# A fused attention and gated-unit kernel: other buffers, a replanned order, and the last stores spread over three queues

## The chip, the cores and the metric

The kernel runs on one core of a Trainium2 chip. The time is device microseconds (us) of one execution; a median is given with its range. The kernel before takes 337.1 us (336.81 to 337.18, four runs).

The engines are called as the profile calls them: PE is TensorE, PEld its weight loads, DVE is VectorE, ACT is ScalarE, POOL is GpSimd, SP is SyncE. A "q" behind a name (POOLq, SPq) is that engine's sequencer, which issues transfers. "The span" is the time from the first to the last instruction in a trace. E is the moment when PE has finished its last matmul.

## The reference, cut to what matters

Eight batches of 576 tokens, eight heads of 64 columns, all in fp32:

```
kv   = einsum('bhsd,bhse->bhde', k, v)          # 64 x 64 per head
out  = einsum('bhsd,bhde->bhse', q, kv)         # "raw" in the kernel
x    = out / sqrt(mean(out^2) + 1e-6) * g_norm  # then heads side by side: (8, 576, 512)
gate = sigmoid(causal convolution of x, 5 taps, per column)
y    = (gate * (x @ w_val)) @ w_out
```

## The kernel before

A planner is given every step with an engine, a wanted time, a duration, and what it needs and frees. It sorts the steps into one order per engine; a table of shifts, found by a search, moves the wanted times. Three parts matter here.

The loads. Half of k (four heads) is one tile; first halves have two buffers (2 - 0), second halves one (2 - 1). All go over SyncE's queue.

```python
    def load_half(name, src, b, i):
        t = loads.tile([P, H // 2, NJ, D], FP32, tag=f"{name}{i}", bufs=2 - i, name=f"{name}{i}_{b}")
        nc.sync.dma_start(out=..., in_=src[b, i * H // 2:(i + 1) * H // 2, 0:SF, :]...)
```

The turn of x. VectorE transposes 32 x 32 blocks into a tile y, and GpSimd's transfers move them into xT.

```python
    def turn_blocks(b, c):
        if ("y", b) not in st:
            st["y", b] = work.tile([P, C // TB, NJ, TB], FP32, tag="y", bufs=1, name=f"y{b}")
        nc.vector.transpose(out=st["y", b][:, :, c, :], in_=...)
```

The stores. A row block of 128 x 512 results (`ot`) leaves in four stores of 64 KB, all over SyncE's queue:

```python
    def store(i, c):
        ot = st["ot", i, c]
        for j in range(HB):                      # HB = 4
            ...
            nc.sync.dma_start(out=rows_out[2 * i + bb, n], in_=ot[j * TB:(j + 1) * TB, :])
```

The last pair of row blocks of the last batch is made by seven products (`fast_product` 0 to 6, lines "cb" and "a" in the profile), whose results ScalarE copies and VectorE adds. One more product ("single", lines "out") makes the last short row block.

Of the kernel before, what the change touches and what calls it, by code (L numbers as in the profile page):

```python
# [18 lines left out]


SHIFTS = {
    "fast_product": {0: -31.5, 1: 1.5, 2: -4},
    "gate_tap": {0: 13, 1: 77, 2: 43, 3: 77, 4: 87, 5: 70.5, 6: 69.5, 7: 67.5},
    "keep_x": {0: -25},
    "kv_product": {5: -4.5, 6: -4.5, 7: -10.5},
    "load_half": {("k", 0): 7.5, ("k", 1): 13.5, ("k", 3): 6.5, ("k", 4): -7, ("k", 5): 34.5,
        ("k", 6): 3.5, ("v", 0): -60.5, ("v", 1): 19.5, ("v", 2): 27.5, ("v", 4): 13, ("v", 5): -9.5,
        ("v", 6): 3, ("v", 7): 9.5},
    "load_q": {4: -11.5, 5: -12, 6: -14.5, 7: -11.5},
    "load_tails": {4: 4.5, 5: -101.5, 6: -108.5},  # L30
    "narrow_weight": {("wout", 0): 36, ("wout", 1): 20.5, ("wout", 3): -39},
    "normalise": {7: 10.5},
    "out_product": {1: 38.5, 3: -6},
    "raw_product": {4: -84, 5: -23, 6: -17.5},
    "square": {2: -9},
    "stage_weight": {("cw", 0): -235.5, ("wout", 0): 13, ("wout", 1): 22, ("wout", 3): -4,
        ("wval", 2): -117, ("wval", 3): -123.5},
    "store": {0: 57.5},
    "sums": {2: 9.5, 5: -91},
    "token_sums": {0: 11.5},  # L40
    "turn_blocks": {6: 23, 7: 9},
    "turn_q": {2: 5.5, 3: 27.5},
    "turn_x": {1: 3, 3: 7.5},
    "val_fast": {7: 12.5},
    "val_product": {0: 33.5, 1: 23, 3: 8.5},
    "weight_sums": {0: 35.5},
    "x_sums": {6: -9},
}


# [85 lines left out]
def kernel(  # L136
# [67 lines left out]
    def ps(kind, shape, name):  # L204
        return psum.tile(shape, FP32, tag=kind, bufs=BANKS[kind], name=name)

    plan = Planner({
        "k0": 2, "k1": 1, "v0": 2, "v1": 1, "tails": 2, "q": 3, "w64": 3, "y": 1, "wexp": 2,
        "kv": 1, "kvbd": 2, "qT": 2, "tp": 1, "raw": 2, "mm": 4, "sq": 2, "ss": 3, "rt": 3,
        "x": 2, "xT": 2, "gate": GATES, "xs": 4, "gv": GVS, "ot": 3,  # L210
    }, by_batch=("tails", "kvbd", "xT", "gv"))
# [42 lines left out]
    st = {}  # L254

    def load_half(name, src, b, i):
        t = loads.tile([P, H // 2, NJ, D], FP32, tag=f"{name}{i}", bufs=2 - i, name=f"{name}{i}_{b}")
        nc.sync.dma_start(
            out=t[:].rearrange("p h j d -> p h (j d)"),
            in_=src[b, i * H // 2:(i + 1) * H // 2, 0:SF, :].rearrange(  # L260
                "h (p j) d -> p h (j d)", j=NJ),
        )
        st[name, b, i] = t
# [277 lines left out]

    def turn_blocks(b, c):
        if ("y", b) not in st:
            st["y", b] = work.tile([P, C // TB, NJ, TB], FP32, tag="y", bufs=1, name=f"y{b}")
        nc.vector.transpose(
            out=st["y", b][:, :, c, :], in_=st["x", b, c][:].rearrange("p (k i) -> p k i", i=TB))

# [194 lines left out]
        else:  # L742
            nc.scalar.copy(out=second[:, LOW], in_=a)

    def store(i, c):
        ot = st["ot", i, c]
        for j in range(HB):
            bb, n = divmod(c * HB + j, NJ * HB) if c < 2 * NJ else (j // 2, NJ * HB + j % 2)
            nc.sync.dma_start(
                out=rows_out[2 * i + bb, n], in_=ot[j * TB:(j + 1) * TB, :])  # L750

    ORDER = [NJ] + list(range(NJ - 1, -1, -1))
    TAPS = range(K - 2, -1, -1)
# [8 lines left out]
    def attention(b, first, step, kv_first, turn_first):  # L762
# [40 lines left out]
        for n, c in enumerate(ORDER):  # L803
            t = first + n * step
            key = b, c
            bank = "mm" if b == 0 and c >= NJ - 2 else "raw"
            end = [("kvbd", b), ("qT", b)] if n == NJ else []
            part = 1.0 if c < NJ else 0.55
            plan.add(
                "PE", 0.87 * part, t, raw_product, b, c,  # L810
                needs=parts + [("kvbd", b)] + before("raw", n, b),
                gives=[("raw", b, c)], takes=[(bank, ("raw", key))], frees=end,
            )
            plan.add(
                "ACT", 0.52 * part, t + 1.0, square, b, c, needs=[("raw", b, c)], gives=[("sq", key)],
                takes=[("sq", key)],
            )
            plan.add(
                "DVE", 0.61 * part, t + 1.6, sums, b, c, needs=[("sq", key)], gives=[("ss", key)],
                takes=[("ss", key)], frees=[("sq", key)],  # L820
            )
            plan.add(
                "POOL", 1.75 * part, t + 2.3, powers, b, c, needs=[("ss", key)], gives=[("rt", key)],
                takes=[("rt", key)], frees=[("ss", key)],
            )
            plan.add(
                "DVE", 0.6 * part, t + 4.2, normalise, b, c, needs=[("raw", b, c), ("rt", key)],
                gives=[("x", key)], takes=[("x", key)], frees=[(bank, ("raw", key)), ("rt", key)],
            )
            if b >= TURNED_X and c < NJ:  # L830
                plan.add(
                    "DVE", 0.63, t + 5.5, turn_blocks, b, c,
                    needs=[("x", key)] + ([("y", b, ORDER[n - 1])] if n > 1 else []),
                    gives=[("y", b, c)], takes=[("y", b)] if n == 1 else [], frees=[("x", key)],
                )
                continue
            plan.add(
                "PE", 0.5 * part, t + 5.5, turn_x, b, c, needs=[("x", key)], gives=[("px", key)],
                takes=[("tp", ("x", key))], frees=[("x", key)],
            )  # L840
            plan.add(
                "ACT", 0.61 * part, t + 6.2, keep_x, b, c, needs=[("px", key)] + before("xT", n, b),
                gives=[("xT", b, c)],
                takes=[("xT", b)] if n == 0 else [], frees=[("tp", ("x", key))],
            )
        t = first + 4 * step + 6.0
        if b >= TURNED_X:
            for n, a in enumerate(range(HB - 1, -1, -1)):
                plan.add(
                    "POOL", 2.4, t + 2.4 * n, move_blocks, b, a,  # L850
                    needs=[("y", b, c) for c in range(NJ)]
                    + [("xT", b, NJ) if n == 0 else ("moved", b, n - 1)],
                    gives=[("xT", b, a), ("moved", b, n)], frees=[("y", b)] if a == 0 else [],
                    load=0.26 / RATE,
                )
            t += 3.0
        plan.add(
# [71 lines left out]
    def products(b, first, step):  # L929
        if b in FAST_VAL:  # L930
            return fast_val(b, first, step * NV * NK / 14)
        made = []
        for jt in range(NK):
            for n in range(NV - 1, -1, -1):
                t = first + (NV * jt + NV - 1 - n) * step
                key = b, jt, n
                plan.add(
                    "PE", 1.93, t, val_product, b, jt, n,
                    needs=[("xT", b, c) for c in HALVES[n]] + [("wval", jt)] + [("val", k) for k in made],
                    gives=[("val", key)],  # L940
                    takes=[("mm", ("val", key))] + ([("gv", b)] if jt == 0 and n == NV - 1 else []),
                )
                plan.add(
                    "ACT", 0.33, t + 2.0, keep_val, b, jt, n, needs=[("val", key)], gives=[("kept val", key)],
                    frees=[("mm", ("val", key))],
                )
                made = [key]
            plan.add(
                "DVE", 0.76, t + 3.0, gated, b, jt,
                needs=[("gate", (b, jt))] + [("kept val", (b, jt, h)) for h in range(NV)]  # L950
                + ([("gv", (b, jt - 1))] if jt else []),
                gives=[("gv", (b, jt))],
                frees=[("gate", (b, jt))] + ([("xT", b)] if jt == NK - 1 else []),
            )
# [4 lines left out]
    def single(b, first):  # L959

        key = b // 2, 2 * NJ
        plan.add(
            "PE", 3.45, first, out_product, *key,
            needs=gated_all(b - 1, b) + [("wout", jt) for jt in range(NK)],
            gives=[("po", key)], takes=[("mm", ("po", key))], frees=[("gv", b - 1), ("gv", b)],
        )
# [9 lines left out]
    def outputs(b, first):  # L976
# [9 lines left out]
        for m in range(2):  # L986
            p = 2 * h + m
            t = first + 6.2 * m
            for n in range(7):
# [2 lines left out]
                own = {2: 0, 4: 2, 5: 1, 6: 4}.get(n)  # L992
                own_sums = {1: 0, 2: 1, 4: 2, 5: 3}.get(n)
                plan.add(
                    "PE", 0.885, t + 0.88 * n, fast_product, *key,
                    needs=used + ([("fast", last)] if last else [])
                    + ([("kept", (i, p, own))] if own is not None else [])
                    + ([("sums", (i, h, own_sums))] if own_sums is not None else [])
# [16 lines left out]
                )  # L1015
            for r, parts in enumerate(((3, 5), (4, 6))):
                chunk = i, 2 * p + r
                plan.add(
                    "SP", 2.0, t + 6.8, store, *chunk, needs=[("kept", (i, p, n)) for n in parts],
                    frees=[("ot", chunk)], load=0.26 / RATE,  # L1020
                )
        if h:
            single(b, first + 12.4)

    def loads_kv(b, want):
        for i in range(2):
# [65 lines left out]
        )  # L1092
    for n in range(4):
        plan.add(
            "DVE", 0.61, begin + 20.0 + n, val_sums, n,
            needs=[("wval", jt) for jt in range(NK)] + ([("vsum", n - 1)] if n else []), gives=[("vsum", n)],
        )
    for b in range(1, B):
# [50 lines left out]
```

## Time and profile before

| | kernel before |
|---|---|
| median of four runs | 337.1 us |
| span of the traced run | 336.3 us |
| PE busy | 319.1 us, 95% |
| first k·v product, first raw, first val | 22.84, 27.66, 42.54 us |
| PE done (E) | 330.46 us |
| from E to the end of the span | 5.84 us |

### The profile page before, as it was taken

What the parts mean: (1) busy time and instruction counts of PE and PEld (TensorE: products, weight loads), DVE (VectorE), ACT (ScalarE), POOL (GpSimd) and SP (SyncE); (2) the same over time, 40 slices, a digit from 0 to 9 for tenths busy, and PEclk for the clock granted to TensorE, in tenths of its full rate; (3) what the DMA queues carried; (4) which work ended last, traced back from release to release, by engine and by line L of the source; (5) the groups of instructions that cost most, each with busy time, mean ns of one, the idle gap of its engine ahead of it and who ended that gap; (6) DMA issues with size and microseconds to landing.
All of it is one profiled execution on the core that took longest, in us unless ns stands there. A gap on an engine that the chain in (4) does not pass through costs nothing.

```text
span 336.3 us, 6403 instructions
## 1 busy us (share of the span) xinstructions
PE 319.1 (95%) x2251; PEld 256.2 (76%) x2251; DVE 281.8 (84%) x504; ACT 151.7 (45%) x325; POOL 140.4 (42%) x178
## 2 busy tenths in 40 slices
PE   2978999999999999999999999999999999999992
PEld 2978878888888878857878877688888577888761
DVE  4535979999999999999788799999989999989601
ACT  5357686585234464352445325343446143534220
POOL 3004603733677438926604478532962193000000
PEclk9999999999999999999999999999999999999999
DMA  6999995699699597577944699622520035220232
GB/s 199 268 305 357 283 248 178 160 251 294 188 232 236 123 259 212 138 209 188 302 111 132 166 258 244 156 55 67 133 63 0 17 87 117 57 55 16 62 95 64
DMA packets 46014, 55.38 MB, mean 165 GB/s; under 512 B 15754, under 2 KB 36254, under 8 KB 45982
## 3 DMA queue, kind: packets, MB, share of 16 engines
q1 hardware_dynamic: 42750, 48.67, 53.9%
q0 software_dynamic: 3072, 6.30, 8.1%
q8 instruction: 18, 0.29, 0.4%
q14 instruction: 14, 0.11, 0.1%
q10 hardware_dynamic: 160, 0.00, 0.0%
HBM read 39.21 MB, written 9.44 MB: 145 GB/s over the span
## 4 chain that ended last, share of the span: by engine, by line
PE 85%; DVE 5%; SPq 4%; DMA 2%; issue 1%; ACT 1%; DVEq 0%; ACTq 0%
PE val L582 19%; PE a L720 14%; PE cb L720 12%; PE raw L484 10%; PE va L632 9%; PE kv L407 6%; PE vc L632 4%; PE out L663 4%; PE vb L632 2%; DMA k<-in_k_dram 2%; PE xTps L530 2%; SPq L267 2%; DVE gate L570 2%; PE qTps L445 1%; SPq L290 1%
## 5 line engine op out<-in xcount | busy, mean ns | idle before, releaser
L512 POOL TENSOR_TENSOR rt<-ss,mhalf 128x8 f32<-128x8 f32 (+1 forms) x40 | 71.0, 1785 | 100.4 <-DVE ss L506 100.3
L570 DVE SCALAR_TENSOR_TENSOR gate<-xT,cwT,gate 128x576 f32<-128x576 f32 x128 | 98.8, 810 | 1.6 <-ACT gate L564 1.3
L553 POOL DMA_DIRECT2D xT<-y x96 | 52.8, 557 | 35.9 <-PE a L720 14.3
L582 PE MATMUL val<-xT,wval 128*128 128x288 f32 x256 | 65.7, 408 | 0.0
L582 PEld LDWEIGHTS val<-xT,wval 128*128 128x128 f32 x256 | 47.6, 190 | 12.9 <-ACT xT L537 0.8
L484 PEld LDWEIGHTS raw<-kvbd,qT 128*128 128x128 f32 (+1 forms) x320 | 35.4, 180 | 6.0 <-issue 2.6
L484 PE MATMUL raw<-kvbd,qT 128*128 128x128 f32 (+1 forms) x320 | 38.9, 280 | 0.8 <-DVE x L520 0.8
L498 ACT ACTIVATE sq<-raw 128x512 f32<-128x512 f32 (+1 forms) x40 | 22.1, 553 | 26.6 <-PE raw L484 26.5
L720 PE MATMUL a<-wsum,sums 128*128 128x256 f32 x128 | 33.5, 384 | 0.6 <-ACT ot L731 0.6
L506 DVE TENSOR_REDUCE ss<-sq 128x8 f32<-128x520 f32 (+1 forms) x40 | 25.3, 633 | 9.7 <-ACT sq L498 9.5
L577 ACT ACTIVATE gate<-gate 128x576 f32<-128x576 f32 x32 | 21.7, 684 | 12.5 <-DVE gate L570 12.3
L720 PEld LDWEIGHTS a<-wsum,sums 128*128 128x128 f32 x128 | 23.7, 190 | 4.7 <-ACT ot L731 1.0
L595 DVE TENSOR_TENSOR gv<-gv,gate 128x576 f32<-128x576 f32 x32 | 23.6, 750 | 2.8 <-ACT gate L577 1.6
L591 ACT COPY gv<-val 128x288 f32<-128x288 f32 x32 | 12.7, 396 | 28.9 <-PE val L582 28.7
L520 DVE TENSOR_TENSOR x<-raw,rt 128x512 f32<-128x512 f32 (+1 forms) x40 | 24.7, 622 | 0.3 <-PE xTps L530 0.3
L729 DVE TENSOR_TENSOR ot<-cb,ot 128x256 f32<-128x256 f32 x32 | 13.4, 420 | 13.7 <-ACT ot L733 9.5
L564 ACT ACTIVATE gate<-xT,cwT 128x576 f32<-128x576 f32 x32 | 23.6, 773 | 1.0 <-DVE gv L595 0.8
L407 PEld LDWEIGHTS kv<-v,k 128*64 128x64 f32 x512 | 17.6, 137 | 6.7 <-issue 5.5
L407 PE MATMUL kv<-v,k 128*64 128x64 f32 x512 | 20.7, 226 | 1.8 <-DMA k<-in_k_dram 1.8
L632 PE MATMUL va<-xs,vsum 128*128 128x288 f32 x64 | 18.1, 406 | 0.0
L720 PE MATMUL cb<-wout,sums 128*128 128x256 f32 x64 | 17.2, 390 | 0.6 <-DVE ot L729 0.2
L720 PE MATMUL cb<-wsum,sums 128*128 128x256 f32 x64 | 16.7, 384 | 0.3 <-DVE sums L696 0.3
(106 smaller groups left out, 510.1 us busy)
## 6 DMA issues: line engine op xcount, KB each, us to landing
q<-in_q_dram SPq DMA_DIRECT2D x96, 140.0 KB, 3.9
out_dram<-ot SPq DMA_DIRECT2D x144, 64.0 KB, 1.7
v<-in_v_dram SPq DMA_DIRECT2D x16, 512.0 KB, 7.3
k<-in_k_dram SPq DMA_DIRECT2D x16, 512.0 KB, 7.5
xT<-y POOLq DMA_DIRECT2D x96, 64.0 KB, 3.6
w_wval<-in_moe_w_val_dram SPq DMA_DIRECT2D x4, 512.0 KB, 6.2
q<-in_q_dram SPq DMA_DIRECT2D x4, 512.0 KB, 8.2
w_wout<-in_moe_w_out_dram SPq DMA_DIRECT2D x4, 512.0 KB, 6.4
```

Source lines behind the costliest of these rows:

```text
L407: nc.tensor.matmul(kvp[r * D:(r + 1) * D, hp, :], st["k", b, half][:, h, j, :] if j < NJ else kl[:, 2 * hp + r, :], st["v", b, half][:, h, ...
L484: nc.tensor.matmul(raw[row * m:(row + 1) * m, col * P:(col + 1) * P], st["qT", b][:, hp, c * P:c * P + m], kv_bd[b % 2][:, hp, :], start=T ...
L506: nc.vector.reduce_sum(out=ss[:, 0:n], in_=st["sq", b, c][:, 0:n], axis=AX.X)
L512: nc.gpsimd.tensor_tensor(out=rt[:, 0:n], in0=st["ss", b, c][:, 0:n], in1=mhalf[:, 0:n], op=ALU.pow)
L520: nc.vector.tensor_tensor(out=x[:, 0:n * D].rearrange("p (h e) -> p h e", h=n), in0=st["raw", b, c][:, 0:n * D].rearrange("p (h e) -> p h ...
L553: nc.gpsimd.dma_start(out=xTs[b % 2][i * TB:(i + 1) * TB, :, first:first + P], in_=y[a * TB:(a + 1) * TB, i])
L564: nc.scalar.activation(out=gate[:], in_=xTs[b % 2][:, jt, HALO:SX], func=AF.Copy, scale=cwT[:, K - 1, jt:jt + 1])
L570: nc.vector.scalar_tensor_tensor(out=gate[:], in0=xTs[b % 2][:, jt, tap * TB:tap * TB + S], scalar=cwT[:, tap, jt:jt + 1], in1=gate[:], op ...
L582: nc.tensor.matmul(val[:], wval[:, kc, jt * P:(jt + 1) * P], xTs[b % 2][:, kc, HALO + n * SV:HALO + (n + 1) * SV], start=(kc == 0), stop=( ...
L595: nc.vector.tensor_tensor(out=both, in0=both, in1=st["gate", b, jt][:], op=ALU.mult)
L632: nc.tensor.matmul(st[bank, "val", b, mj][:], weights_[:, k], tokens()[:, k], start=(n in (0, 1, 3) and k == 0), stop=(k == NK // 2 - 1), ...
L720: nc.tensor.matmul(st[bank, i, p], tokens()[:, k], weights_[:, k], start=(n < 2 and k == 0), stop=(k == NK // 2 - 1), skip_group_check=True)
```

## The change

Its intent: give y a second buffer and pay for it with the second buffers of the first k and v halves; search the order again with durations corrected from a trace; and spread the stores of the last pair over three queues, so that SyncE need not issue them one after the other.

```diff
 SHIFTS = {
-    "fast_product": {0: -31.5, 1: 1.5, 2: -4},
...                                                  # the whole table is new
+    "load_half": {("k", 0): -105.5, ("k", 3): 4.5, ("k", 4): -12, ("k", 6): -27.5, ("v", 0): -11.5,
...
-        "k0": 2, "k1": 1, "v0": 2, "v1": 1, "tails": 2, "q": 3, "w64": 3, "y": 1, "wexp": 2,
+        "k0": 1, "k1": 1, "v0": 1, "v1": 1, "tails": 2, "q": 3, "w64": 3, "y": 2, "wexp": 2,
...
-        t = loads.tile([P, H // 2, NJ, D], FP32, tag=f"{name}{i}", bufs=2 - i, name=f"{name}{i}_{b}")
+        t = loads.tile([P, H // 2, NJ, D], FP32, tag=f"{name}{i}", bufs=1, name=f"{name}{i}_{b}")
...
-            st["y", b] = work.tile([P, C // TB, NJ, TB], FP32, tag="y", bufs=1, name=f"y{b}")
+            st["y", b] = work.tile([P, C // TB, NJ, TB], FP32, tag="y", bufs=2, name=f"y{b}")
...
-                "PE", 0.87 * part, t, raw_product, b, c,
+                "PE", 0.905 * (1.0 if c < NJ else 0.62), t, raw_product, b, c,
...                                                  # and five more durations of the plan, by 1 to 23%
+                if b == B - 1 and m:
+                    last_stores(chunk, r, t + 6.8)
+                    continue
...
+    def last_stores(chunk, r, want):
+
+        kept = lambda n: ("kept", (chunk[0], 3, n))
+        if r == 0:
+            plan.add(
+                "POOL", 2.4, want, store, *chunk, slice(0, C), (nc.gpsimd,), needs=[kept(3), kept(5)],
+                frees=[("ot", chunk)], load=0.26 / RATE,
+            )
+            return
+        plan.add(
+            "SP", 2.0, want, store, *chunk, HIGH, (nc.sync,), needs=[kept(4)], frees=[("ot", chunk)],
+            load=0.13 / RATE,
+        )
+        plan.add(
+            "SP", 1.0, want + 1.0, store, *chunk, LOW, (nc.sync, nc.scalar), needs=[kept(6)],
+            frees=[("ot", chunk)], load=0.13 / RATE,
+        )
...
-            "DVE", 0.61, begin + 20.0 + n, val_sums, n,
+            "DVE", 0.61, 150.0 + n, val_sums, n,
```

More of the change, by code (lines that the diff above doesn't have):

```diff
@@ L21 @@
 SHIFTS = {
-    "fast_product": {0: -31.5, 1: 1.5, 2: -4},
-    "gate_tap": {0: 13, 1: 77, 2: 43, 3: 77, 4: 87, 5: 70.5, 6: 69.5, 7: 67.5},
-    "keep_x": {0: -25},
-    "kv_product": {5: -4.5, 6: -4.5, 7: -10.5},
-    "load_half": {("k", 0): 7.5, ("k", 1): 13.5, ("k", 3): 6.5, ("k", 4): -7, ("k", 5): 34.5,
-        ("k", 6): 3.5, ("v", 0): -60.5, ("v", 1): 19.5, ("v", 2): 27.5, ("v", 4): 13, ("v", 5): -9.5,
-        ("v", 6): 3, ("v", 7): 9.5},
-    "load_q": {4: -11.5, 5: -12, 6: -14.5, 7: -11.5},
@@ L30 @@
-    "load_tails": {4: 4.5, 5: -101.5, 6: -108.5},
-    "narrow_weight": {("wout", 0): 36, ("wout", 1): 20.5, ("wout", 3): -39},
-    "normalise": {7: 10.5},
-    "out_product": {1: 38.5, 3: -6},
-    "raw_product": {4: -84, 5: -23, 6: -17.5},
-    "square": {2: -9},
-    "stage_weight": {("cw", 0): -235.5, ("wout", 0): 13, ("wout", 1): 22, ("wout", 3): -4,
-        ("wval", 2): -117, ("wval", 3): -123.5},
-    "store": {0: 57.5},
-    "sums": {2: 9.5, 5: -91},
-    "token_sums": {0: 11.5},
-    "turn_blocks": {6: 23, 7: 9},
@@ L42 @@
-    "turn_q": {2: 5.5, 3: 27.5},
-    "turn_x": {1: 3, 3: 7.5},
-    "val_fast": {7: 12.5},
-    "val_product": {0: 33.5, 1: 23, 3: 8.5},
-    "weight_sums": {0: 35.5},
-    "x_sums": {6: -9},
+    "fast_keep": {3: 8},
+    "fast_product": {1: -15, 3: -3.5},
+    "gate_tap": {0: 30, 1: 40.5, 2: 66, 3: 64, 4: 72.5, 5: 53, 6: 56, 7: 32.5},
+    "kv_product": {2: 48.5, 5: 19.5},
+    "load_half": {("k", 0): -105.5, ("k", 3): 4.5, ("k", 4): -12, ("k", 6): -27.5, ("v", 0): -11.5,
+        ("v", 4): -13, ("v", 5): -11, ("v", 7): -9.5},
@@ new lines @@
+    "load_q": {2: -6, 5: 2, 6: -30, 7: -22},
+    "load_q_rows": {0: -16},
+    "load_tails": {4: -1.5, 5: 0.5, 7: -0.5},
+    "move_blocks": {3: 22.5},
+    "narrow_weight": {("wout", 1): 6, ("wout", 2): 6, ("wout", 3): 7.5, ("wval", 0): -19,
+        ("wval", 1): -26.5, ("wval", 2): 14},
+    "normalise": {2: 12, 7: -20},
+    "out_product": {1: -28},
+    "raw_product": {4: -1.5},
+    "stage_weight": {("cw", 0): -102, ("wout", 1): 30.5, ("wout", 2): 7, ("wout", 3): 57, ("wval", 1): 3,
+        ("wval", 2): -109, ("wval", 3): -93},
@@ L48 @@
+    "sums": {2: 16.5, 3: -3.5, 4: -37.5, 5: 11.5, 7: 24.5},
+    "token_sums": {0: -31.5},
+    "turn_blocks": {6: -13, 7: 1},
+    "turn_q": {2: 16.5, 3: 11.5},
+    "turn_x": {1: 11.5, 6: 14},
+    "val_fast": {4: 38, 7: 9},
+    "val_keep": {6: -64},
+    "val_product": {0: 11, 1: 10.5, 2: 34.5, 3: 34.5},
+    "val_sums": {1: 41},
+    "x_sums": {6: 16},
 }
@@ L743, in fast_keep, with store @@
             nc.scalar.copy(out=second[:, LOW], in_=a)
-    def store(i, c):
+    def store(i, c, cols=slice(0, C), queues=(nc.sync,)):
         ot = st["ot", i, c]
@@ L748, in store @@
             bb, n = divmod(c * HB + j, NJ * HB) if c < 2 * NJ else (j // 2, NJ * HB + j % 2)
-            nc.sync.dma_start(
-                out=rows_out[2 * i + bb, n], in_=ot[j * TB:(j + 1) * TB, :])
+            queues[j % len(queues)].dma_start(
+                out=rows_out[2 * i + bb, n, :, cols], in_=ot[j * TB:(j + 1) * TB, cols])
     ORDER = [NJ] + list(range(NJ - 1, -1, -1))
@@ L822, in attention @@
             plan.add(
-                "POOL", 1.75 * part, t + 2.3, powers, b, c, needs=[("ss", key)], gives=[("rt", key)],
+                "POOL", 1.82 * part, t + 2.3, powers, b, c, needs=[("ss", key)], gives=[("rt", key)],
                 takes=[("rt", key)], frees=[("ss", key)],
@@ L853, in attention @@
                     gives=[("xT", b, a), ("moved", b, n)], frees=[("y", b)] if a == 0 else [],
-                    load=0.26 / RATE,
+                    load=0.32 / RATE,
                 )
@@ L937, in products @@
                 plan.add(
-                    "PE", 1.93, t, val_product, b, jt, n,
+                    "PE", 1.95, t, val_product, b, jt, n,
                     needs=[("xT", b, c) for c in HALVES[n]] + [("wval", jt)] + [("val", k) for k in made],
@@ L962, in single @@
         plan.add(
-            "PE", 3.45, first, out_product, *key,
+            "PE", 3.6, first, out_product, *key,
             needs=gated_all(b - 1, b) + [("wout", jt) for jt in range(NK)],
@@ L994, in outputs @@
                 plan.add(
-                    "PE", 0.885, t + 0.88 * n, fast_product, *key,
+                    "PE", 0.9, t + 0.88 * n, fast_product, *key,
                     needs=used + ([("fast", last)] if last else [])
```

## The prediction

> **What bounds the kernel now.** I read the page's busy shares first, then the slices, then TensorE's instructions in order of time at the two ends.
>
> ```profile
> span 336.3 us, 6403 instructions
> PE 319.1 (95%) x2251; PEld 256.2 (76%) x2251; DVE 281.8 (84%) x504; ACT 151.7 (45%) x325; POOL 140.4 (42%) x178
> PE   2978999999999999999999999999999999999992
> DVE  4535979999999999999788799999989999989601
> DMA  6999995699699597577944699622520035220232
> ```
>
> TensorE (PE) is busy 319.1 of 336.3 us, and its idle time lies in the first and last slices. The change gives it no less work (the same matmuls, but for those that only keep it warm), so only time that is not useful work can go. Summed over stretches from 40 to 310 us, PE's idle time is about 2 us, and the waits that the profile names there are 0.8 us at most. The middle has nothing large to win. The head does:
>
> ```profile
> 6.26 0.26 PE L377 MATMUL cwps<-ident,cw 20*128 20x20 f32 x1 [6.26 <-DVE cw L355]
> 6.45 5.87 PE L396 MATMUL kv<-ident 128*128 128x128 f32 x32
> 12.34 0.68 PE L445 MATMUL qTps<-ident,q 64*64 64x64 f32 x16
> 12.95 2.50 PE L396 MATMUL kv<-ident 128*128 128x128 f32 x20
> 15.38 3.71 PE L445 MATMUL qTps<-ident,q 128*64 128x128 f32 x64
> 19.02 2.05 PE L396 MATMUL kv<-ident 128*128 128x128 f32 x16
> 22.84 0.69 PE L407 MATMUL kv<-v,k 128*64 128x64 f32 x16 [1.76 <-DMA k<-in_k_dram]
> ...
> 26.80 0.94 PE L396 MATMUL kv<-ident 128*128 128x128 f32 x6 [0.85 <-ACT kvbd L417]
> 27.66 4.42 PE L484 MATMUL raw<-kvbd,qT 128*64 128x128 f32 x40
> ...
> 42.54 2.21 PE L582 MATMUL val<-xT,wval 128*128 128x288 f32 x8
> ```
>
> The lines of L396 multiply the identity only to keep the engine warm: they are busy, but idle time in truth. Of the first 22.84 us only 4.5 are work (0.26, about 0.6 and 3.65 us): PE waits for the transfer of k. From the first k·v product to "raw" are 4.89 us, for 2.63 us of products. From raw to the first val are 14.9 us, with 2.0 us of warming matmuls among them. From 42.5 us on PE never starves. At the other end:
>
> ```profile
> 328.45 0.73 PEld L720 LDWEIGHTS cb<-wout,sums 128*128 128x128 f32 x4 [0.50 <-DVE ot L729]
> 328.45 1.13 PE L720 MATMUL cb<-wout,sums 128*128 128x256 f32 x4
> 329.42 1.03 PE L720 MATMUL a<-wsum,gv 128*128 128x256 f32 x4
> ...
> 330.48 0.37 ACT L743 COPY ot<-a 128x256 f32<-128x256 f32 x1 [2.54 <-PE a L720]
> ```
>
> PE is done at 330.46 and the span ends at 336.3: 5.84 us in which only stores run. The last eight, seen by their tensor in that window:
>
> ```profile
> L749 SPq DMA_DIRECT2D out_dram<-ot x8: 314/424/428, 330.1 to 333.2; - x8
> DMA to landing us min/median/max: 1.7/1.7/1.7
> ```
>
> The last store is issued at 333.2, lands 1.7 us later at 334.9, and 1.4 us of closing follow. One queue issuing eight stores costs more than the landing.
>
> **What the Trainium skill says.** "Perfetto Trace Analysis", section "Identifying the Most-Contended Engine", warns that matmul busy time is a poor measure of the distance from the roofline. The trace agrees: part of the 95% is warming. "DMA: Bandwidth & Descriptors", section "Issuing engines are not separate DMA queues", says that issuing from several engines only saves issue time, since all use the same 16 DMA engines. That is just what the tail lacks: about 0.42 us of issue each on one queue, with DMA engines two tenths busy. "TensorE: Matmul & The Clock Gate", section "Part 1: The HAM clock gate", says that an idle window of about 3.4 us halves the clock. The records grant 1.00 even in the first 10 us, but the first 32 warming records take 5.87/32 = 0.183 us each against 2.50/20 = 0.125 later, so I allow for a slow restart. No page bears on how many buffers this kernel needs.
>
> **Part 1, buffers.** Half a k or v tile is 4 KB per partition; giving up the second buffer of the first halves frees 8 KB, what a second y takes. No instruction disappears. In the trace VectorE's transposes into y wait 0.0 us for anything, so the second y buys nothing by itself; it gives the ordering freedom. The danger is in k and v: a load may now start only when the last product with the old half is done. I took the order of the changed kernel and added up the PE work between the place where each load is planned and its first product. The smallest gap after the start is 12.3 us (second halves of batch 4), the rest 14 to 35 us; the page shows 7.3 to 7.5 us median to land. In the kernel before the smallest gaps are 3.8 and 4.2 us without a wait in the trace. So I charge nothing.
>
> **Part 2, the head.** The new order issues k0, k1 directly after the first weight, and v0, v1 after the first q; a wout load moves behind them. Landing times read from the kernel before, with bytes issued so far: weight 0.54 MB at 5.2 us, second weight 1.07 at 7.9, short q 2.25 at 12.3, both q 3.30 by 15.4, wout 4.34 at 20.3, k0 4.87 at 22.7, third weight 5.92 at 26.0. From the second weight to the short q that is 0.27 MB/us. The four tails and wout took 5.0 us from 15.3; less 0.52/0.27 = 1.9 for wout, the tails take 3.1.
> - After: the same 3.30 MB by 15.3, two v (1.05/0.27 = 3.9) and half the tails (1.5): k, v and tails are there at about 20.7. PE has fewer warming matmuls (21 before kv instead of 34 or so), but idles from about 5 us to 12 and may run slowly then; I take 21.0. Gain 1.8.
> - kv to raw: 2.63 of products, 0.76 for the two ACT copies, about 0.3 start: 3.7 instead of 4.89, raw at 24.7 instead of 27.7. Gain 1.2. A q transposition of 0.6 us now stands inside that wait.
> - raw to val: raw 4.36, eight warming matmuls 1.2, xT 0.22 + 3 x 0.59, q turned 4 x 1.02, half of kv 1.32: 12.95 us. The second batch's q may be late: 20.7 + 1.5 (other tails) + 0.8 (short q) + 1.57/0.3 (three weights) + 1.05/0.3 = 31.7, needed at 24.7 + 6.6 = 31.3, so 0.4 of wait. Val starts at about 38.1, with one xT (0.59) left for later: as good as 38.7 against 42.6.
> - Sum of the head: 3.9 us.
>
> **Part 3, the tail.** The last single product (3.58 us) moves between the fifth and sixth product of the last pair. The wait for ot ahead of 328.45, with its slower start, is covered: 0.5 us. Then, with E the end of PE: the first row block goes over GpSimd's queue from E-0.4 (the sixth product ends at E-0.88, VectorE's add takes 0.42). GpSimd's own transfers in the trace:
>
> ```profile
> L553 POOL DMA_DIRECT2D xT<-y x16: 548/551/593, 269.1 to 279.8; - x16
> DMA to landing us min/median/max: 1.9/2.0/2.1
> ```
>
> Four of 0.55 us: the last starts at E+1.25 and lands at E+3.25. SP has the half block early, the four of the single product by E+0.6, then two half stores, landed by E+2.7; ACT's two by E+2.5. End: E+3.25+1.4 = E+4.65 instead of E+5.84, gain 1.2. With the 0.5 it is 1.7; I count 1.6, as GpSimd has not yet stored to HBM in this trace.
>
> **Part 4, the middle.** VectorE is close behind PE: between 30 and 310 us it is busy 261.3 of 280 us (93%). One wout narrowing (five operations, 2.9 us) leaves its idle time at 20 to 25.5 us, where it cost nothing, for the full stretch, and the stretch gets some 3.5 us shorter: 264.2/276.5 = 95.5%. The four vsum additions (2.7 us) go to later, which helps the first gates. Counting PE work against VectorE work ahead of each use of the token sums, the tightest places lead by 3.5 us before and 3.4 after. I charge 0.3 us.
>
> **Sum.** 337.1 - 3.9 - 1.6 + 0.3 = 331.9; I say 331.8.
>
> **Rivals.** (a) VectorE becomes the bound once the head is shorter: its 93% speaks for it, the equal lead against. Each 1% lost there gives back 2.8 us: 333 to 336. (b) k and v with one buffer make PE wait: the late issue speaks for it, the gaps of 12 us and more against. Two waits of 2 us would give 336. (c) GpSimd's stores are slower than its SBUF transfers: over all of its 96 transfers the landing is 3.6 us median. Then the tail gains only 0.5: 333. (d) PE's restart or the second batch's q takes the place of the wait for k: 333 to 334. (e) The corrected durations also remove the waits and slow starts of the middle, some 3 us by the gaps between matmul groups: 329.
>
> **Range and chances.** The two ends are well founded, and their errors are about 1 us each; the reordered middle adds about 1.5 either way, with more room for loss. 8 in 10: 329.3 to 335.0. Two per cent faster is 330.4, which takes nearly all of (e): 0.27. Slower by 2% would be 343.9, a failure of the middle by 12 us: 0.01.
>
> **What would show it.** Right: the first kv product at about 21 us, raw near 24.7, val near 38, PE done about 4.5 us earlier, no DMA wait of PE for k or v after the first, and 4.5 to 5 us between PE's end and the span's. Wrong: named PE waits on k, v or q loads after 40 us; VectorE at full tenths with PE waiting for sums, gv or x; or stores of GpSimd landing more than 3 us after issue.

## More of the kernel before

At the start, matmuls of the identity with itself keep PE warm while it waits for data; they fill only the time after a planned moment:

```python
        idle_from = 9.0
        for start, step in plan.order():
            if step["engine"] == "PE" and start < 60.0:
                keep_warm(int((start - idle_from) / 0.3))
                idle_from = start + step["time"]
            step["fn"](*step["args"])
```

The trace cut into stretches shows where each engine works. Columns: the stretch, its length, the busy time of PE, PEld, DVE, ACT and POOL (instructions in brackets), the granted PE clock as a share of full speed, the share of the 16 DMA engines that is busy, and GB/s.

```profile
core 0: us, PE busy (x) PEld busy (x) DVE busy (x) ACT busy (x) POOL busy (x), PEclk, DMA share, GB/s
0.00:10.00 10.00, 3.74 (x17) 3.73 (x18) 5.62 (x29) 6.20 (x10) 2.68 (x10) 1.00 0.76 220
10.00:20.00 10.00, 9.99 (x126) 9.44 (x125) 3.15 (x6) 3.98 (x15) 0.00 (x0) 1.00 1.17 261
45.00:320.00 275.00, 272.72 (x1768) 217.83 (x1763) 254.21 (x436) 122.06 (x257) 128.04 (x159) 1.00 0.58 150
330.00:337.00 7.00, 0.44 (x3) 0.04 (x1) 0.04 (x1) 0.37 (x1) 0.00 (x0) 0.86 0.29 75
```

The third row is the bulk: PE works 272.7 of 275 us there, VectorE 254.2. In the last row hardly anything computes any more (PE 0.44 us, one copy of ScalarE), but transfers still run at 75 GB/s: these are the last stores. In the first row PE works little, and much of what it does in the second is warming.

## The result, and the profile after

The changed kernel takes 338.35 us (338.22 to 338.96, four runs), against 337.1 of before in the same rounds. Ratios here and below are the mean time of one kernel's fast runs over that of the other's in the same rounds, so not quite the ratio of the medians: here it is 1.0042, with a 95% interval of 1.0025 to 1.006. The change makes the kernel slightly slower, well inside 2%, and 6.6 us slower than the 331.8 us predicted; the range of 329.3 to 335.0 does not hold it.

First the page of the changed kernel: the span, the busy shares, and four rows of slices (each digit the busy share of one fortieth of the span, in tenths).

```profile
span 336.1 us, 6353 instructions
PE 315.5 (94%) x2221; PEld 253.6 (75%) x2221; DVE 279.0 (83%) x504; ACT 150.5 (45%) x325; POOL 139.5 (41%) x182
PE   5599999999999999999999999999999999999970
POOL 3006523534467659676003328866344670000020
PEclk9599999999999999999999999999999999999996
DMA  6999979792698689899749568225400333122230
```

Read the right-hand end. PE's last digits are 7 and 0: in the last slice of 8.4 us it does nothing at all. The DMA row ends in 0 too. So it is not a store that the end waits for: no data moves any more. POOL has a 2 in the last slice but one: GpSimd's stores, of which the kernel before had none. At the left-hand end the clock has a 5 where it was 9.

PE's instructions in order of time at the head of the changed kernel: start, busy time, engine, line, operation, out<-in, shapes, count, and in brackets the idle time just before with what ended it.

```profile
1.36 4.21 PE L397 MATMUL kv<-ident 128*128 128x128 f32 x18 [1.36 <-POOL ident masks.py:199]
12.15 1.12 PE L446 MATMUL qTps<-ident,q 64*64 64x64 f32 x16 [6.58 <-DMA q<-in_q_dram]
13.42 3.56 PE L397 MATMUL kv<-ident 128*128 128x128 f32 x18
...
21.42 0.69 PE L408 MATMUL kv<-v,k 128*64 128x64 f32 x16
...
25.24 4.43 PE L485 MATMUL raw<-kvbd,qT 128*64 128x128 f32 x40
...
38.41 2.21 PE L583 MATMUL val<-xT,wval 128*128 128x288 f32 x8
```

The first k·v product, raw and val start at 21.42, 25.24 and 38.41 us; 21.0, 24.7 and 38.1 were predicted. The kernel no longer waits for k. It waits 6.58 us for q instead and restarts slowly: 18 warming matmuls take 3.56 us, 0.198 each, against 0.125 in a warm stretch of before (2.50/20). The granted clock in this trace is low there, as the first of these two stretches shows (columns as above):

```profile
10.00:20.00 10.00, 7.84 (x91) 7.57 (x93) 6.72 (x16) 7.12 (x18) 0.00 (x0) 0.69 1.19 266
330.00:337.00 7.00, 0.00 (x0) 0.00 (x0) 0.00 (x0) 0.00 (x0) 0.00 (x0) 0.51 0.00 0
```

The clock alone is no sure sign of a slow restart. In hw_tail, a kernel below with the same order and the same rest before q, it reads 1.00 from 10 to 20 us, and the 18 warming matmuls are slower still (4.16 us, 0.231 each).

The second row is the end: zeros for every engine and for the transfers, where the same stretch of before still had stores. All engines at the tail of the changed kernel, in order of time:

```profile
324.17 1.03 PE L721 MATMUL a<-wsum,gv 128*128 128x256 f32 x4
324.37 0.42 DVE L730 TENSOR_TENSOR ot<-cb,ot 128x256 f32<-128x256 f32 x1 [4.16 <-PE cb L721]
325.09 1.99 POOL L750 DMA_DIRECT2D out_dram<-ot  x4 [50.26 <-DVE ot L730]
325.23 0.37 ACT L744 COPY ot<-a 128x256 f32<-128x256 f32 x1 [1.28 <-PE a L721]
325.64 0.83 ACTq L750 DMA_DIRECT2D out_dram<-ot  x2
```

PE is done at 325.20 us, 5.3 us earlier than in the first trace of before. GpSimd wakes after 50.26 us of rest, issues four stores and is done at 327.08. By the view of transfers these four land 2.2 us (median) after their issue, so all data is in memory by about 329. The span ends at 336.1.

What fills the rest is not counted as busy and is in none of these views: closing instructions, which the trace puts down to the line that opens the kernel's outermost context (`with _tile.TileContext(nc) as tc:`, L1166 here, L1144 in the kernel before). Asked for by that line, they give, for the changed kernel (operation and count, min/median/max duration in ns, first and last start in us):

```profile
L1166 POOLq DRAIN  x3: 34/102/8913, 326.4 to 335.8; - x3
L1166 SPq DRAIN  x3: 7/7/7, 329.1 to 335.6; - x3
L1166 PEldq DRAIN  x2: 13/2354/4695, 320.5 to 335.6; - x2
```

and for the kernel before, with GpSimd's last work above them:

```profile
276.02 4.34 POOL L553 DMA_DIRECT2D xT<-y  x8
...
L1144 POOLq DRAIN  x3: 34/102/11568, 276.7 to 336.0; - x3
L1144 SPq DRAIN  x3: 7/7/7, 335.5 to 335.8; - x3
```

By these rows each engine's sequencer drains that engine and then meets the others. PE's first drain, 4.695 us from 320.5 on, ends at 325.2, with PE's last matmul. GpSimd's does not end with its last work. After the change, GpSimd's first drain starts at 326.4 and lasts 8.913 us, to 335.3: 8.2 us beyond GpSimd's last store. SyncE reached its own first drain at 329.1, with its stores landed, and its next ones start only when GpSimd is there. From 329.1 to 335.3 the core waits for GpSimd: 6.2 us. (The view of waits puts 6.3 us of SyncE's down to PE's sequencer, whose drain was long over; the end of GpSimd's drain and the experiments below say GpSimd.) In the kernel before, GpSimd's last work ends at 276.02 + 4.34 = 280.36, its drain at 276.7 + 11.568 = 288.3, also about 8 us later, but 47 us before anyone needs it. There GpSimd works without a pause from 269.07 on, so a long rest before the last work is not what brings the 8 us.

### The profile page after: what moved, and what is told of

Read it like the earlier page. It is cut to its first block, busy times and chain, and to the rows that moved or that the text cites. A ratio compares the mean times of both kernels' runs of the same rounds, so it can differ in the third digit from the quotient of the medians.

```text
span 336.1 us, 6353 instructions
## 1 busy us (share of the span) xinstructions
PE 315.5 (94%) x2221; PEld 253.6 (75%) x2221; DVE 279.0 (83%) x504; ACT 150.5 (45%) x325; POOL 139.5 (41%) x182
## 4 chain that ended last, share of the span: by engine, by line
PE 87%; DMA 4%; DVE 3%; SPq 1%; ACT 1%; issue 1%; POOL 0%; POOLq 0%; DVEq 0%
PE val L583 19%; PE a L721 15%; PE cb L721 12%; PE raw L485 10%; PE va L633 9%; PE kv L408 6%; PE vc L633 4%; PE out L664 4%; DMA q<-in_q_dram 3%; PE qTps L446 3%; PE vb L633 2%; PE kv L397 2%; PE xTps L531 2%; DVE gate L571 1%; DMA vl<-in_v_dram 1%
## 5 line engine op out<-in xcount | busy, mean ns | idle before, releaser
L513 POOL TENSOR_TENSOR rt<-ss,mhalf 128x8 f32<-128x8 f32 (+1 forms) x40 | 68.0, 1706 | 117.3 <-DVE ss L507 117.2
L750 POOL DMA_DIRECT2D out_dram<-ot x4 | 2.0, 503 | 50.3 <-DVE ot L730 50.3
```

The lines of the kernel that those rows point to most:

```text
L513: nc.gpsimd.tensor_tensor(out=rt[:, 0:n], in0=st["ss", b, c][:, 0:n], in1=mhalf[:, 0:n], op=ALU.pow)
```

## The experiments

Theory A: whatever GpSimd does last, its closing drain ends some 8 us later, and the change put that on the path that sets the end. Two forms: A1, only GpSimd's own transfers bring it; A2, any instruction of GpSimd does. Rivals: B, the stores themselves are slow; C, the new order or the buffers cost time elsewhere. Eleven runs follow, one of them the kernel before once more; each gave a correct result. The medians beside a result are those of before in the same call (three calls, each on one chip).

### Moving GpSimd's four stores to SyncE and ScalarE (hw_tail)

```diff
-                "POOL", 2.4, want, store, *chunk, slice(0, C), (nc.gpsimd,), needs=[kept(3), kept(5)],
+                "SP", 1.0, want, store, *chunk, slice(0, C), (nc.sync, nc.scalar), needs=[kept(3), kept(5)],
```

> The changed kernel, but the four stores that it gives to GpSimd's queue go to SP's and ACT's, two each; every matmul as before. Theory A (GpSimd's closing drain, 8.9 us in the trace of the changed kernel, cannot end until about 8 us after its last transfer): the drain is hidden again, SP's last store is issued at about 327, lands at 329, closing 1.4 us, so the span is about 330.5 instead of 336.1 and the time about 332.7 us. Theory B (the stores themselves or the use of three queues are slow): no gain over 1 us, 337 to 339. Theory C (the new order of the middle lost what the head won): 337 to 339 as well, and PE ends later than 325.

Measured: 333.84 us (332.85 to 334.51) against 336.96; ratio 0.9899 [0.9876, 0.9923]. PE's order is that of the changed kernel, and E is 325.77. The last stores and the drain:

```profile
L750 SPq DMA_DIRECT2D out_dram<-ot x10: 314/420/429, 321.6 to 328.0; - x10
...
L1166 POOLq DRAIN  x3: 34/102/10353, 273.0 to 330.4; - x3
L1166 SPq DRAIN  x3: 7/7/7, 329.9 to 330.2; - x3
```

GpSimd's last work is now the turn of the last x, ending at 275.40, and the drain ends at 283.4. From E to the end of the span are 4.9 us instead of 10.9. One line of queue choice was worth 4.5 us (338.35 to 333.84; the two medians are of different calls). It speaks for A and against C; B, as that text has it, expected no gain either. The median is 1.1 us above what A expected (332.7); the traced run, 332.85, is not.

### The order of the change with the old stores (sp_tail)

```diff
-                if b == B - 1 and m:
+                if False:
                     last_stores(chunk, r, t + 6.8)
```

> The changed kernel with the old last stores: all whole rows on SP's queue. A: no late transfer of GpSimd, but 12 stores of 0.42 us one after the other from 324.0: the last issued at about 328.7, landed at 330.5, span about 332, time about 334.3 us; so halves over two queues are worth about 1.6 us and the new order of head and middle with the old tail about 3 us. B: 333 to 335 too (no GpSimd), so this run tells only against C, which expects 337 or more.

Measured: 334.94 us (334.76 to 335.54), ratio 0.9937 [0.992, 0.9954]. E is 325.72, and the last of SyncE's stores is issued at 329.6, so 6.9 us pass from E to the end. The new order alone is thus worth 2.0 us by the medians, although it makes the old tail 1 us worse than the 5.84 of before: the "single" product now ends late, and its four stores queue up with the eight others. Splitting the queue takes this from 6.9 to 4.9.

### The kernel before with four last stores on GpSimd (before_pool)

```diff
+                if b == B - 1 and m and r == 0:
+                    plan.add(
+                        "POOL", 2.4, t + 6.8, store, *chunk, nc.gpsimd,
+                        needs=[("kept", (i, p, n)) for n in parts], frees=[("ot", chunk)], load=0.26 / RATE,
+                    )
+                    continue
```

> The kernel before with one edit: the four stores of the last pair's first row block go to GpSimd's queue, at 330.3 to 332.3. A: the drain ends about 8.3 us after that, at 340.6, and closing brings the span to about 341.3, 5 us more than before: time about 342 us. B (slow stores or contention in the changed kernel alone) or the prediction's own account of the tail: 335.5 to 337.

Measured: 342.74 us (341.96 to 343.69), ratio 1.0171 [1.0142, 1.0199].

```profile
329.59 1.99 POOL L749 DMA_DIRECT2D out_dram<-ot  x4 [49.97 <-DVE ot L729]
...
L1150 POOLq DRAIN  x3: 34/102/8915, 330.9 to 340.3; - x3
```

The cost comes with GpSimd's stores into a kernel that has neither the new order nor the new buffers. The drain, 8915 ns, is that of the changed kernel to 2 ns, and from E (329.70) to the end are again 10.9 us. Theory C is out for this cost.

### A small GpSimd copy in place of the stores, twice (pool_copy, pool_copy_late)

A1 and A2 differ if GpSimd does something late that is not a transfer. Both kernels are hw_tail with a copy of eight columns added on GpSimd.

```diff
+    def touch(i, c):
+        nc.gpsimd.tensor_copy(touched[:], st["ot", i, c][:, 0:H])          # pool_copy
+        nc.gpsimd.tensor_copy(touched[:], st["ot", i, c][:, C - H:C])      # pool_copy_late, instead
```

> hw_tail plus one small GpSimd copy (128x8) that waits for the same VectorE add as GpSimd's stores did, so that GpSimd computes late but moves nothing late. A in its narrow form (the drain waits for transfers): as hw_tail, within 0.5 us. Rival (any late GpSimd instruction puts a drain of 8 us behind itself): drain until about 333.5, span about 334.2, 3.7 us more than hw_tail.

Measured: 332.97 us (332.82 to 333.24), ratio 0.9876 [0.9862, 0.9891]. The test was flawed: the columns that it reads are finished early, so the copy ran at 320.14 and not at E. Nor is it explained that the median is 0.9 us below hw_tail's, with one instruction more; so no difference of under 1 us between two kernels' medians is read here as an effect.

```profile
320.14 0.19 POOL L755 COPY touched<-ot 128x8 f32<-128x8 f32 x1 [43.92 <-DVE ot L731]
...
L1173 POOLq DRAIN  x3: 34/102/8143, 320.1 to 330.6; - x3
```

Its drain lasted 8.143 us all the same, to 328.2, and was hidden behind the stores. So the time could not tell A1 from A2; the drain's own row already could. The second kernel reads columns that VectorE's last addition writes.

> pool_copy mended: in that run the small copy read a half of the tile that is finished early, so it ran at 320.1 and its drain, 8.1 us long, was hidden; it tested nothing. Here it reads the half that VectorE's last add writes, so it runs at about 325.3. Theory A2 (whatever GpSimd does last, about 8 us of drain follow): drain until about 333.5, span about 334.2 and 3 us slower than hw_tail, about 336.3. Theory A1 (only its transfers bring the drain): as hw_tail, span 330.7 to 331.5.

Measured: 336.33 us (335.87 to 336.99) against 337.18, ratio 0.9973 [0.9959, 0.9988].

```profile
324.82 0.19 POOL L755 COPY touched<-ot 128x8 f32<-128x8 f32 x1 [50.03 <-DVE ot L731]
...
L1173 POOLq DRAIN  x3: 34/102/8145, 324.8 to 333.5; - x3
L1173 SPq DRAIN  x3: 7/7/7, 329.3 to 333.2; - x3
```

A copy of 0.19 us, whose result nobody uses, makes the kernel 2.5 us slower than hw_tail's median: SyncE is ready at 329.3, GpSimd at 324.8 + 8.145 = 332.9. By the traced spans (333.7 and 330.7) it is 3.0 us, as A2 expected. A2 holds, A1 falls, and B with it: this kernel's late GpSimd work stores nothing.

### One GpSimd store instead of four (one_pool)

```diff
-                "POOL", 2.4, want, store, *chunk, slice(0, C), (nc.gpsimd,), needs=[kept(3), kept(5)],
+                "POOL", 0.6, want, store, *chunk, slice(0, C), (nc.gpsimd, nc.sync, nc.scalar, nc.sync), ...
```

> The changed kernel with one of GpSimd's four last stores left on its queue, the other three on SP and ACT. If the drain is a fixed cost after the last GpSimd instruction: the one store ends near 325.7, the drain near 333.8, span about 334.5, only 1.5 us less than the changed kernel. If the drain grows with the number of late transfers (8.3 us for four): a drain of 2 to 3 us, hidden, and a span of about 330.7.

Measured in one run (state unknown): 337.48 us, span 335.4.

```profile
326.06 0.52 POOL L750 DMA_DIRECT2D out_dram<-ot  x1 [50.27 <-DVE ot L730]
...
L1166 POOLq DRAIN  x3: 34/102/8543, 326.0 to 335.1; - x3
```

The drain ends at 334.5, 8.0 us after the store's end. From E to the end are 9.2 us instead of 10.9: the tail is 1.7 us shorter, since GpSimd's last store ends 1.5 us sooner after E (0.4 us after it instead of 1.9). So it is a fixed cost after the last instruction, not one per transfer. The head of this run was 1 us slower, at a clock of 0.58 from 10 to 20 us, so the total is worth less than the row.

### A warm head (hw_warm), and both ideas together (best)

The changed order lets PE rest 6.5 us before q and restart slowly. Here hw_tail gets 29 instead of 9 identity products (two matmul records each) ahead of the first q; "best" also shares the last stores more evenly.

```diff
-        idle_from = 9.0
+        idle_from = 3.0
```

> hw_tail with 29 instead of 9 identity products at the start, so that TensorE does not idle from 5.6 to 12.1 us. If the idle time is what lowers the granted clock to 0.69 between 10 and 20 us: clock 0.95 or more there, the first q transposition 0.7 us instead of 1.1, the 18 records of warming 2.3 instead of 3.5, and the first kv product at about 19.8 instead of 21.4, unless a load comes later; span 329 to 329.5 and 1 to 2 us faster than hw_tail, with less spread. If the clock is low for another reason, or loads bind at 21 us anyway: no change within 0.4 us.

Measured: 333.7 us (331.94 to 333.96, five runs), ratio 0.9882 [0.9862, 0.9901]: no gain over hw_tail, where 1 to 2 us were expected. The head did improve, as expected: the first q transposition took 0.68 us instead of 1.12, the 18 warming matmuls after it 2.27 instead of 4.16, and the first k·v product began at 19.50 instead of 21.93. So the rest does slow the restart. The granted clock doesn't tell the two kernels apart: from 10 to 20 us it reads 1.00 in both. Val began at 37.06 instead of 38.92 in hw_tail, 1.9 us earlier. But E was 325.84, against 325.77. The waits of PE (who waited for whom: us in total, times, longest) show two that hw_tail has not, or has at 0.3 us:

```profile
PE cb L721 <- DVE sums L697: 1.1, 2, 0.8
...
PE raw L485 <- DVE x L521: 0.6, 1, 0.6
```

Between val and E lie 288.8 us here, and 286.8 to 286.9 in the changed kernel, hw_tail and hw_even. PE now waits 1.4 us longer for VectorE's results by these two lines, most of the 1.9 us lost; "best", which has the warm head too, shows the same two waits, 1.1 and 0.6. So VectorE seems to leave this order no room for a shorter head; no run that relieves VectorE tests it.

> hw_warm with the last 14 stores shared evenly: SP and ACT take two each of the single product, three and one of the first row block, two each of the last halves. SP's last issue ends about 1.4 us earlier than in hw_tail, so 1 to 1.5 us less than hw_warm: span about 328, time about 330.3 us, close to 2% below the kernel before. If landing or closing binds instead: as hw_warm.

The edit in "best", beside the warm head:

```diff
-            "SP", 2.0, first + 4.3, store, *key, needs=[("ot", key)], frees=[("ot", key)],
+            "SP", 2.0 if b < B - 1 else 0.8, first + 4.3, store, *key, slice(0, C),
+            (nc.sync, nc.scalar) if b == B - 1 else (nc.sync,), needs=[("ot", key)], frees=[("ot", key)],
...
-                "SP", 1.0, want, store, *chunk, slice(0, C), (nc.sync, nc.scalar), needs=[kept(3), kept(5)],
+                "SP", 1.0, want, store, *chunk, slice(0, C), (nc.sync, nc.scalar, nc.sync, nc.sync), ...
```

Measured: 332.55 us (331.22 to 334.3, six runs), ratio 0.9861 [0.9836, 0.9886]. It beats both kernels, but two edits were in it.

### A second trace of before, the split alone, and the even sharing alone (before_again, before_split, hw_even)

The traced run of before took 338.08 us, 1 us above its median, so the gains read against that trace may be too large.

> The kernel before, unchanged, to get a second trace of it: the profiled run of the first trace took 338.08 us where the median is 337.1, and its span of 336.3 us is about 1 us longer than those of its other runs (334.9 to 336.2, mostly 335.2 to 335.5). Theory: the first trace fell about 1 us slow, so comparing spans overstates the gain of the head and tail by that much. Expected then: span about 335.3, TensorE done at about 329.5 instead of 330.46, the GpSimd drain hidden as before. Rival: the difference lies after TensorE's end; then TensorE is done at 330.4 again and the tail is 1 us shorter.

Measured: 337.38 us, span 335.6 (one run, state unknown; before's median in this call was 337.55). The k·v products and PE's last matmul in this second trace:

```profile
22.13 0.69 PE L407 MATMUL kv<-v,k 128*64 128x64 f32 x16 [0.60 <-DMA k<-in_k_dram]
...
328.71 1.03 PE L720 MATMUL a<-wsum,gv 128*128 128x256 f32 x4
```

The wait for k is 0.60 us here, 1.76 in the first trace, and everything after it is 0.7 us earlier: raw 26.96, val 41.83, E 329.74. From val to E it is 287.9 us in both traces. So the first trace overstated the head that there was to win, by 0.7 us.

The split of the last pair's stores over two queues, in the kernel before, without GpSimd. The edit stands in the loop over both row blocks, so it moves four stores to ScalarE, two of each block, and not two of the last block alone, as the expectation says:

```diff
+                if b == B - 1 and m:
+                    for queue, rows, more in ((nc.sync, (0, 1), []), (nc.scalar, (2, 3), [("kept", (i, p, 6))])):
+                        plan.add("SP", 1.0, t + 6.8, store, *chunk, queue, rows, ...)
+                    continue
```

> The kernel before with nothing changed but the last row block's four stores: two on SyncE, two on ScalarE, none on GpSimd. It takes the change's idea for the tail alone, without its cost. Theory (the split is worth its issue time, the drain of GpSimd is all that spoils it): two fewer issues of 0.42 us behind one another on SyncE, so 0.8 us or a little more less than before, about 336.2. Rival (the split gains nothing, the landing sets the end anyway): within 0.2 us of before, about 337.1.

Measured: 336.2 us (335.42 to 336.61) against 337.55, ratio 0.9963 [0.9931, 0.9995].

```profile
L749 SPq DMA_DIRECT2D out_dram<-ot x10: 314/421/428, 322.0 to 330.1; - x10
L749 ACTq DMA_DIRECT2D out_dram<-ot x4: 364/408/453, 329.2 to 330.6; - x4
```

ScalarE's queue has four stores in the trace, so SyncE has four fewer, 1.7 us of issue. From E (329.14) to the end of the span are 4.5 us instead of 5.84. The idea behind the change's tail is sound: issue time on one queue was the cost, and sharing it gains about 1.4 us in the trace, if GpSimd isn't one of the queues. That the median is the expected 336.2 is luck in part, since the expectation counted two moved stores.

The even sharing alone is "best" with `idle_from = 9.0` as in the change.

> The changed kernel without a late GpSimd store, the last stores shared more evenly over SyncE and ScalarE, and the head as in the change (few warming matmuls). It separates the two edits of the fastest kernel so far (332.55 us). If the even sharing is what helped: about 332.7, 1 us below the 333.8 of the plain move to SyncE and ScalarE. If the warm head helped: about 333.8.

Measured: 332.27 us (331.68 to 332.72), ratio 0.9841 [0.9813, 0.987]. This is the fastest of all kernels here by its median ("best" is within the spread), 1.6% faster than before, and it has no warm head. From E (326.29) to the end are 4.3 us, against 4.9 in hw_tail. In "best" val starts 2 us earlier than here, at about 37.5 against 39.50, and E is 326.31 against 326.29: the warm head brings nothing, a second time.

### All of them together

| kernel | median us | ratio to before | E | end of span | between |
|---|---|---|---|---|---|
| before, first trace | 337.1 | 1 | 330.46 | 336.3 | 5.8 |
| before_again | 337.38 (1 run) | – | 329.74 | 335.6 | 5.9 |
| the change | 338.35 | 1.0042 | 325.20 | 336.1 | 10.9 |
| before_pool | 342.74 | 1.0171 | 329.70 | 340.6 | 10.9 |
| one_pool | 337.48 (1 run) | – | 326.17 | 335.4 | 9.2 |
| pool_copy_late | 336.33 | 0.9973 | 325.16 | 333.7 | 8.5 |
| pool_copy | 332.97 | 0.9876 | 325.93 | 330.9 | 5.0 |
| sp_tail | 334.94 | 0.9937 | 325.72 | 332.6 | 6.9 |
| hw_tail | 333.84 | 0.9899 | 325.77 | 330.7 | 4.9 |
| hw_warm | 333.7 | 0.9882 | 325.84 | 330.8 | 5.0 |
| best | 332.55 | 0.9861 | 326.31 | 330.6 | 4.3 |
| before_split | 336.2 | 0.9963 | 329.14 | 333.6 | 4.5 |
| hw_even | 332.27 | 0.9841 | 326.29 | 330.6 | 4.3 |

The buffers were not tried by themselves. With a single y tile the changed order, kept as it is, deadlocks when it is built; with second buffers for k0 and v0 beside the two y, the tiles don't fit (63.94 KB wanted, 60.09 KB left per partition). Two neighbours do build, but were not run: the changed table with the planner told of one y, which gives another order, and the kernel before with one buffer for each first half of k and v. What each buffer count is worth stays open.

## Why the prediction was wrong, point by point

**The step that failed** is in Part 3: "End: E+3.25+1.4 = E+4.65 instead of E+5.84, gain 1.2." Its 3.25 was nearly right: the last of GpSimd's stores was issued at 326.6, E+1.4, and landed 2.2 us later, at about E+3.6. The 1.4 was wrong. It was read off the kernel before as "closing", as if the closing began when the last data had landed, whoever moved it. In these traces each engine closes for itself, and GpSimd's closing ends about 8 us after its last instruction. The end was E+10.9. The trace gives the size without any experiment: 335.3 - 329.1 = 6.2 us in which SyncE and its landed stores waited for GpSimd's drain. Without these the span would end at 329.9, E+4.7 (329.1 and the 0.8 us that follow the drain, 335.3 to 336.1), and the time would be 338.35 - 6.2 = 332.2, against 331.8 predicted. hw_tail (333.84) and hw_even (332.27) are inside the predicted range.

**Rival (c)** looked at the right engine and the wrong duration. It asked whether GpSimd's stores land late. They landed in 2.2 us, and its 333 us did not come. The prediction's own test, "4.5 to 5 us between PE's end and the span's", did find the error.

**Could it have been seen before?** Yes. The kernel before has the same drain, 11.568 us from 276.7 on, ending 7.9 us after GpSimd's last work. It cost nothing there, stands in no busy time, no slice and no group, and I didn't ask for it. A change that gives an idle engine the last work should have led there.

**Part 2, the head**, held in its times, but in part by luck. It took the first k·v product from the loads (20.7) and allowed 0.3 us for a slow restart. In the trace no load of k or v binds: from q's landing at 12.1 us on PE works without a wait, and its slow restart sets 21.42; with a warm PE (hw_warm) it was 19.50. The slow restart after a rest agrees with the page on the clock gate that the prediction names: between 10 and 16 us the changed kernel's records grant 0.50. But hw_tail's grant 1.00 after the same rest, so its record does not show the slowness. One sum is off: from the first k·v product to raw were 4.82 us (27.66 - 22.84), not 4.89. As gains the terms were too large, since the trace of before was a slow one: from 42.54 to 38.1 are 4.4 us, but against the second trace of before val came 3.4 us earlier.

**Part 1, the buffers**, held: no wait of PE for k or v is named in the changed kernel, so rival (b) did not occur. Rival (d) came true in its first half: PE's restart took the place of the wait for k, though at 0.4 us beyond the 21.0. No wait for the second batch's q is named.

**Part 4, the middle**: the charge of 0.3 us was not seen. From val to E the changed kernel takes 286.8 us and before 287.9, though one transposition of 0.59 moved into that stretch; the covered wait of 0.5 us is part of the gain; what the rest is, no run tells apart. Rival (a), VectorE as the bound, is not active in the changed kernel, but it seems close: in hw_warm PE's waits for VectorE grew by 1.4 of the 1.9 us that the warm head had gained.

**The balance.** Against the second trace of before, E came 4.54 us earlier (329.74 to 325.20; about 4.5 was predicted) and the tail grew by 5.0 (5.9 to 10.9): the span grew by 0.5 us. The medians differ by 1.25. Of the rest, 0.34 lies outside the span: time minus span is 1.78 us for before_again and 2.12 for the changed kernel (2.15 for hw_tail and 1.78 for before_pool, so it is not the drain). Its cause stays open. The remaining 0.4 is within what runs of one kernel differ by; the spans of before range from 334.9 to 336.8 us.

## What to carry to other kernels

Before you give the last work of a kernel to an engine that has long been idle, ask the trace when that engine's closing instructions end, and not only when its transfers land. Here GpSimd must have done its last instruction, be it a store or a small copy, about 8 us before the last store lands; sharing issue time between SyncE and ScalarE gave the relief without that cost. And when a shorter head brings no shorter kernel, measure the stretch from the head to the end: if it has grown by as much, the next bound is there.

## What the Trainium skill lacked or had wrong

- "VectorE: DVE Perf Modes", section "The DRAIN you can't avoid", knows the drain after each VectorE instruction and those that the runtime adds around a kernel, about 12 ns each, constant, on all five engines. The first closing drains here, which bear the kernel's own line, are neither. PE's lasts until PE's last matmul (4695 ns in the changed kernel). GpSimd's lasts 8143 to 11578 ns in these runs and ends 7.9 to 8.2 us after its last instruction, whether that was a copy of 0.19 us, one store or four. What the drain does in that time no run here shows.
- "Runtime: NRT & Kernel Launch", section "The ~15µs preamble/postamble breakdown", gives about 1.5 us to the runtime's closing barrier, which waits for all engines. The meeting of the engines at the kernel's own line is not in its table. Before, 1.4 us passed from the last landing to the end of the span; after, SyncE stood there from 329.1 to 336.1, 7.0 us, for GpSimd had worked last.
- "DMA: Bandwidth & Descriptors", section "Issuing engines are not separate DMA queues", says that issuing from several engines only saves issue time. It did: 1.4 us over two queues in before_split. That a late GpSimd queue costs 6.2 us at the end is on neither this page nor another that I found. Section "Anatomy of one DMA — SWDGE (gpsimd) path" of the same page has about 2.0 us plus bytes over 436 GB/s for a GpSimd transfer, so 2.15 us for 64 KB by that formula (an estimate); the runs agree with 2.2.
